# Integer additions of a weight conversion on VectorE, and one block's second product in unsplit float32

## The chip, the cores and the metric

The kernel runs on one core of a Trainium2 chip. What counts is the device time of one launch in microseconds. The engines are TensorE (PE, with its weight loads as PEld), VectorE (DVE), ScalarE (ACT), GpSimd (POOL) and SyncE (SP), which issues most transfers.

## The reference

Three layers follow each other, on 1536 tokens of width 512. The change touches the middle one.

```python
attn_out = _attn_ref(q, k, v)            # 2 x 8 heads, 768 positions: a window of +-15 and 24 block sums
x = attn_out, heads joined               # 1536 x 512
h = x @ w_in                             # 512 x 2048, "first product"
g = where(h > 0, h, exp(min(h, 0)) - 1)
x = g @ w_out                            # 2048 x 512, "second product"
# then a layer of 8 experts, one for each token:
#   e = argmax(x @ w_gate);  out = weight * (relu(x @ w1[e]) @ w2[e])
```

The weights `w_in` and `w_out` arrive in 64-bit floats, and the kernel makes 32-bit ones of them.

## The kernel before

**Blocks and chunks.** The tokens go through attention and the first layer in four blocks of 512, 256, 384 and 384 (`UNITS` counts units of 64 queries). A block j runs over 16 chunks c of 128 hidden columns: `mm_h` (the first product, L422), `elu` (three ScalarE and two VectorE instructions, L433 to L437, with the result `elp`), and, two chunks later, `mm_y` (the second product, L467), which adds into one PSUM bank for each 128 tokens. Attention of the next block's units is put between these steps: scores (L309), the masked maximum (L319), exponent, normalisation (L361), turn (L371), weighted sum (L392), and then the high and the low part of x (`xh` on ScalarE, `xl` on VectorE, L398 and L405). One PSUM buffer `T` serves turns, weighted sums and the means of v.

**Products in parts.** A float32r operand keeps fewer digits than a float32 one. The first product takes x and the weights each as a high and a low part and adds three float32r products. The second product does the same with `split_g` (g into `gh` and `gl`, L447 and L448) and `split_w` (w_out into two parts `wsp`, L175 and L176). In the first block, for chunks below `C3`, it is one float32 product of `elp` and `wo` with no split; there `elp` takes the buffers of `gh` and `gl`, two of each, odd chunks one kind and even chunks the other.

**Conversion.** For each of the 16 chunks both weights are converted, 32 pieces of 128 by 512. A piece takes a ScalarE instruction on the lower half-words (`conv_r`, L127), two VectorE instructions on the upper ones (`conv_t`, L138 and L139), and an integer addition of both (`conv_f`, L146). A piece of w_in then goes through a ScalarE rounding (`conv_h`, L152) and a subtraction (`conv_l`, L157) into high and low part.

**Order.** The start-up is written out by hand in `START`: attention of the first block and the conversion of the first pieces (C00, C01, C10, C20, C30, C11, C21: seven additions; E0 to E3: four subtractions). After it the loop over the 64 steps issues, in each step, the conversion of two pieces, some three chunks ahead of their use; the framework's scheduler puts each engine's instructions of this part into an order by its own timeline, before the run. In the run each engine takes its queue in order. The last block and the experts follow an order of their own.

Of the kernel before, what the change touches and what calls it, by code (L numbers as in the profile page):

```python
# [9 lines left out]
F32 = mybir.dt.float32  # L10
# [5 lines left out]
ALU = mybir.AluOpType  # L16
# [19 lines left out]
BLK = [j for j in range(NBLK) for _ in range(UNITS[j])]  # L36
NF = FF // 128
NS = 6
C3 = 8
WARM = 22  # L40
AT0 = (2, -2, 1)
ATS = (5, 4, 5)
# [14 lines left out]
EXD = (3, 5)  # L57
EXP = (0, 1, 2, 3, 4, 6, 7)
NORMD = (0, 4, 7)
LOE = "VVVPVV"  # L60
START = "w23 w43 x3 w53 w03 w13 w33 w51 x1 w31 w21 w11 w41 w01 w52 x2 w22 w02 w12 w42 w50 x0 w00 w20 w32 d2 d0 w40 d5 k2 s0 w30 d3 k4 k1 k3 s2 k0 k5 m0 w10 s5 m2 e0 s3 m5 M0 e2 m3 d4 M1 r0 b5 d1 b3 s4 n0 e5 r2 t0 e3 m4 n2 s1 c0 z3 e4 M2 z5 t2 r3 r5 M3 n3 c2 m1 A00 M4 n5 B00 e1 M5 k6 r4 C00 n4 t5 P s6 r1 c5 p1 n1 A01 p6 t4 p2 D0 o5 B01 c4 o2 h5 k7 m6 t3 C01 h2 s7 c3 E0 e6 t1 p7 m7 p0 A10 r6 o0 c1 p3 n6 p4 e7 o3 l5 B10 o1 t6 h3 r7 h0 C10 l3 c6 n7 o4 A11 l0 h1 t7 B20 h4 o6 A20 c7 l1 C20 h6 l4 o7 D1 l2 l6 H0 h7 E1 D2 l7 A30 B30 E2 C30 H1 B11 C11 D3 A21 B21 E3 C21"
HID = (5, 10, 15)
LOP = (1, 3, 5, 8, 10, 12, 14)
# [16 lines left out]
class Prog:  # L80
# [60 lines left out]
    def conv_f(self, c, part):  # L141
        t2, r = self.cv.pop((c, part))
        f = t2
        if part == 1:
            f = self.wo[:, c].bitcast(I32)
        self.nc.gpsimd.tensor_tensor(f, t2, r, op=ALU.add)  # L146
        self.w[c, part] = f

    def conv_h(self, c):
# [4 lines left out]

    def conv_l(self, c):
        w, f = self.w[c, 0], self.cvf.pop(c)
        (self.nc.gpsimd if LOE[c % len(LOE)] == "P" else self.nc.vector).tensor_tensor(w[:, 1], f, w[:, 0].bitcast(F32), op=ALU.subtract)  # L157

    def conv_a(self, c, part):
        self.conv_r(c, part)  # L160
# [8 lines left out]
    def split_w(self, j, c):  # L169
        if j == 0 and c < C3:  # L170
            return
        nc = self.nc
        f = self.w[c, 1].bitcast(F32)
        w = self.ws.tile([128, 2, 512], F32R, tag="ws", name="wsp")
        nc.scalar.copy(w[:, 0], f)  # L175
        nc.vector.tensor_tensor(w[:, 1], f, w[:, 0].bitcast(F32), op=ALU.subtract)  # L176
        self.wsp[j, c] = w
# [247 lines left out]
    def elu(self, j, c):  # L425
# [4 lines left out]

        pool, tag = (self.gp, "gh" if c % 2 else "gl") if j == 0 and c < C3 else (self.el, "p")
        p = pool.tile([128, TB], F32, tag=tag, name="elp")[:, :TBS[j]]
# [7 lines left out]
    def split_g(self, j, c):  # L440
        nc = self.nc
        if j == 0 and c < C3:
            return
# [13 lines left out]
    def mm_y1(self, j, c, t):  # L457
        nc = self.nc
        g = self.g[j, c]
        sl = slice(t * 128, t * 128 + 128)  # L460
        if j == 0 and c < C3:
            ops = ((g, self.w[c, 1].bitcast(F32)),)
# [74 lines left out]
    def part1(self):  # L537
# [31 lines left out]
        for x in ORDER.split():  # L569
            f = dict(q=self.load_q, n=self.load_v0, v=self.load_v, w=wload, k=self.load_k0, c=self.load_c)[x[0]]  # L570
            f(int(x[1:]))
        self.new_x(0)
        self.new_x(1)
        self.start_up()
        conv_done = [x for x in pieces if x in self.w]
        del cq[:len(conv_done)]
        while dq and dq[0] in self.split:
# [66 lines left out]
        for i in range(len(steps)):  # L644
            run(2 * i)
            j, c = steps[i]
# [19 lines left out]
    def start_up(self):  # L666

        unit = dict(d=self.diag_q, k=self.k_sum, s=self.scores, m=self.maxes, b=self.less_max, e=self.at1b, z=self.sums, r=self.recip, n=self.norm,
                    t=self.turn, c=self.turned, o=self.weighted, h=self.x_hi, l=self.at5, p=self.v_pad, x=self.max_k0, M=self.mean_v0)
        part = dict(A=self.conv_r, B=self.conv_t, C=self.conv_f)  # L670
        self.split, self.half = set(), set()
        with self.tc.manual_schedule():
            for op in START.split():
                if op[0] == "H":
                    self.mm_h(0, int(op[1:]), 0, TB // 2)
                    self.half.add(int(op[1:]))
                    continue
                k, n = op[0], [int(i) for i in op[1:]]
                if k in unit:
                    unit[k](*n)  # L680
                elif k in part:
                    part[k](*n)
                    if k == "C" and n[1] == 1:
                        self.split.add((n[0], 1))
                elif k == "w":
                    self.window(*n)
                elif k == "P":
                    self.pad_v0()
                elif k == "D":
                    self.conv_h(*n)  # L690
                elif k == "E":
                    self.conv_l(*n)
                    self.split.add((n[0], 0))
# [805 lines left out]
```

## Time and profile before

| | us |
|---|---|
| time, median of 3 runs | 567.46 (567.41 to 567.75) |
| profiled execution, its time | 567.08 |
| its span, first to last instruction | 565.3 |
| busy: TensorE, VectorE, ScalarE, GpSimd | 538.3, 366.3, 311.4, 115.7 |

The profile is of one execution. Times in it are counted from the span's start. A matmul's end is modelled, and matmuls overlap, so that the price of a product is read from the starts of what follows it. The granted clock is that of TensorE, 1.00 being full speed.

### The profile page before, as it was taken

The page shows a single profiled execution, that of the slowest core. Times are in us where ns is not written, and L with a number is a line of the kernel's source. Part 1 is how long each engine was busy: PE and PEld are TensorE (multiplying, and loading weights), DVE is VectorE, ACT ScalarE, POOL GpSimd, SP SyncE. Part 2 cuts the span into 40 slices and gives each one's busy share as a digit, 9 for nine tenths or more (in the row PEclk, how much of TensorE's full clock was granted, in tenths as well). Part 3 has the DMA queues.
Part 4 walks back from the last instruction along what each step waited for, and adds up shares of the span by engine and source line. Part 5 has one row for each costly group of instructions (what it writes and reads, how often), then busy time and mean ns, then how long its engine had stood idle before and what let it go on. Part 6 is the DMA issues. An engine that isn't in the chain of part 4 may idle for free. (4 is left out here: it accounts for less than half of the span.)

```text
span 565.3 us, 9614 instructions
## 1 busy us (share of the span) xinstructions
PE 538.3 (95%) x3113; PEld 422.5 (75%) x3113; DVE 366.3 (65%) x966; ACT 311.4 (55%) x768; POOL 115.7 (20%) x139
## 2 busy tenths in 40 slices
PE   8877998789999999999999999999999999999995
PEld 4465664557889888988888989877888665675884
DVE  6999899997647886787565778885741100444510
ACT  5775564546557877775665754673232222565620
POOL 3656365434000000000000000431432111100001
PEclk9979999889999999999999999998999999999999
DMA  9999733342114130310100101541077979593611
GB/s 291 317 353 399 239 139 105 123 133 52 57 48 138 49 93 16 118 48 14 48 2 1 56 1 50 170 118 56 19 221 267 382 260 370 162 379 131 237 56 40
DMA packets 38714, 81.33 MB, mean 144 GB/s; under 512 B 4095, under 2 KB 8575, under 8 KB 38656
## 3 DMA queue, kind: packets, MB, share of 16 engines
q1 hardware_dynamic: 36336, 73.30, 38.8%
q0 software_dynamic: 2320, 7.34, 3.8%
q8 instruction: 26, 0.43, 0.3%
q14 instruction: 32, 0.26, 0.1%
HBM read 103.70 MB, written 6.55 MB: 195 GB/s over the span
## 5 line engine op out<-in xcount | busy, mean ns | idle before, releaser
L422 PE MATMUL h<-xh,wi 128*128 128x384 f32 (+2 forms) x528 | 144.6, 342 | 0.2 <-ACT elp L435 0.2
L467 PE MATMUL y<-wsp,gh 128*128 128x512 f32 x320 | 100.9, 403 | 0.3
L422 PEld LDWEIGHTS h<-xh,wi 128*128 128x128 f32 x528 | 93.6, 189 | 8.3 <-ACT elp L435 1.0
L422 PE MATMUL h<-xl,wi 128*128 128x384 f32 (+2 forms) x264 | 88.0, 333 | 0.0
L467 PEld LDWEIGHTS y<-wsp,gh 128*128 128x128 f32 x320 | 58.2, 191 | 10.5 <-ACT gh L447 1.1
L467 PE MATMUL y<-wsp,gl 128*128 128x512 f32 x160 | 62.3, 405 | 1.3 <-DVE gl L448 1.3
L1157 DVE TENSOR_TENSOR holdl<-S,holdh 128x512 fp32r<-128x512 f32 x22 | 15.2, 689 | 72.1 <-ACT holdh L1153 53.7
L1125 PE MATMUL h<-w2s,holdh 128*128 128x512 f32 x176 | 61.0, 407 | 0.0
L1168 PE MATMUL y<-w2s,holdh 128*128 128x512 f32 x176 | 59.1, 398 | 0.0
L436 DVE SCALAR_TENSOR_TENSOR elt<-ele,elt 128x384 f32<-128x384 f32 (+2 forms) x64 | 41.3, 646 | 19.5 <-ACT ele L434 19.1
L422 PEld LDWEIGHTS h<-xl,wi 128*128 128x128 f32 x264 | 49.9, 189 | 4.5 <-issue 1.2
L433 ACT ACTIVATE elt<-h 128x384 f32<-128x384 f32 (+2 forms) x64 | 31.4, 491 | 28.5 <-PE h L422 23.0
L447 ACT CAST gh<-elp 128x384 fp32r<-128x384 f32 (+2 forms) x56 | 27.8, 496 | 31.9 <-DVE elp L437 22.0
L176 DVE TENSOR_TENSOR wsp<-wo,wsp 128x512 fp32r<-128x512 f32 x56 | 39.9, 713 | 8.2 <-ACT wsp L175 7.5
L437 DVE SCALAR_TENSOR_TENSOR elp<-elt,elp 128x384 f32<-128x384 f32 (+2 forms) x64 | 41.8, 652 | 3.9
L175 ACT CAST wsp<-wo 128x512 fp32r<-128x512 f32 x56 | 34.7, 620 | 15.4 <-PE y L467 13.8
L1125 PEld LDWEIGHTS h<-w2s,holdh 128*128 128x128 f32 x176 | 33.9, 192 | 8.3 <-issue 0.8
L336 ACT ACTIVATE e<-e,nb 128x120 f32<-128x120 f32 x88 | 33.7, 389 | 10.4 <-DVE nb L324 10.2
L1168 PEld LDWEIGHTS y<-w2s,holdh 128*128 128x128 f32 x176 | 33.1, 188 | 8.4 <-issue 1.6
L448 DVE TENSOR_TENSOR gl<-elp,gh 128x384 fp32r<-128x384 f32 (+2 forms) x56 | 31.0, 554 | 12.1 <-ACT gh L447 10.8
L467 PEld LDWEIGHTS y<-wsp,gl 128*128 128x128 f32 x160 | 29.9, 190 | 8.4 <-DVE gl L448 2.5
L1125 PE MATMUL h<-w2s,holdl 128*128 128x512 f32 x88 | 35.0, 398 | 0.0
(290 smaller groups left out, 973.1 us busy)
## 6 DMA issues: line engine op xcount, KB each, us to landing
wo<-in_w SPq DMA_DIRECT2D x9, 2048.0 KB
wo<-in_w SPq DMA_DIRECT2D x18, 1024.0 KB
ri<-in_w_in SPq DMA_DIRECT2D x16, 512.0 KB
ro<-in_w_out SPq DMA_DIRECT2D x16, 512.0 KB
wo<-in_w SPq DMA_DIRECT2D x32, 256.0 KB
w2p<-in_w SPq DMA_DIRECT2D x32, 256.0 KB
w2q<-in_w SPq DMA_DIRECT2D x24, 256.0 KB
q<-in_q SPq DMA_DIRECT2D x18, 256.0 KB
```

Source lines behind the costliest of these rows:

```text
L175: nc.scalar.copy(w[:, 0], f)
L176: nc.vector.tensor_tensor(w[:, 1], f, w[:, 0].bitcast(F32), op=ALU.subtract)
L336: nc.scalar.activation(e[:, p], e[:, p], AF.Exp, bias=nb[:, p:p + 1], scale=0.125, accum_out=sm[:, p:p + 1])
L422: nc.tensor.matmul(h, lhsT=w[:, wl, k * 128:k * 128 + 128], rhs=x[:, k, a:b], start=(n == 0), stop=(n == 11))
L433: nc.scalar.activation(t, h, AF.Tanh, scale=0.5)
L436: nc.vector.scalar_tensor_tensor(t, e, 1.0, t, op0=ALU.add, op1=ALU.mult)
L437: nc.vector.scalar_tensor_tensor(p, t, 0.0, p, op0=ALU.min, op1=ALU.add)
L447: nc.scalar.copy(gh, p)
L448: nc.vector.tensor_tensor(gl, p, gh.bitcast(F32), op=ALU.subtract)
L467: nc.tensor.matmul(self.y[j][t], lhsT=gx[:, sl], rhs=wx, start=(c == 0 and n == 0), stop=(c == NF - 1 and n == len(ops) - 1))
L1125: nc.tensor.matmul(self.h[s, hf], lhsT=x[:, k], rhs=w, start=(n == 0), stop=(n == 11))
L1168: nc.tensor.matmul(self.y2[s], lhsT=g[:, ks], rhs=w, start=(i == 0 and n == 0), stop=(i == 7 and n == 2))
```

## The change

`C3` goes from 8 to 16, so that the first block's second product is one float32 product in all 16 chunks, with no split of g and of w_out there. The integer addition of a conversion is made on VectorE instead of GpSimd, but for the seven of the start-up. The subtractions of the conversion that were on GpSimd (chunks 3, 9 and 15, the first of them in the start-up) are made on VectorE like the others.

```diff
-C3 = 8
+C3 = 16
...
-LOE = "VVVPVV"
...
     def conv_f(self, c, part):
...
-        self.nc.gpsimd.tensor_tensor(f, t2, r, op=ALU.add)
+        (self.nc.gpsimd if self.early else self.nc.vector).tensor_tensor(f, t2, r, op=ALU.add)
         self.w[c, part] = f
...
     def conv_l(self, c):
         w, f = self.w[c, 0], self.cvf.pop(c)
-        (self.nc.gpsimd if LOE[c % len(LOE)] == "P" else self.nc.vector).tensor_tensor(w[:, 1], f, w[:, 0].bitcast(F32), op=ALU.subtract)
+        self.nc.vector.tensor_tensor(w[:, 1], f, w[:, 0].bitcast(F32), op=ALU.subtract)
...
         self.start_up()
+        self.early = False
...
-        self.split, self.half = set(), set()
+        self.split, self.half, self.early = set(), set(), True
```

## Rows read from the trace of the kernel before

**Rows 1.** The page: its span, and busy time, share and instructions of VectorE.

```profile
span 565.3 us, 9614 instructions
...
PE 538.3 (95%) x3113; PEld 422.5 (75%) x3113; DVE 366.3 (65%) x966; ACT 311.4 (55%) x768; POOL 115.7 (20%) x139
```

**Rows 2.** Busy time by stretches: from:to, length, engines (instructions), clock, DMA, GB/s.

```profile
53.00:140.00 87.00, 77.73 (x331) 50.82 (x332) 80.77 (x140) 51.20 (x117) 40.51 (x29) 0.94 0.44 144
...
55.00:60.00 5.00, 5.00 (x13) 2.69 (x12) 4.90 (x8) 4.37 (x14) 3.04 (x3) 0.73 1.04 297
...
75.00:80.00 5.00, 5.00 (x21) 2.93 (x20) 5.00 (x9) 1.71 (x3) 2.67 (x2) 1.00 0.32 105
...
100.00:105.00 5.00, 3.72 (x15) 3.02 (x16) 4.96 (x7) 2.83 (x6) 2.59 (x2) 0.70 0.20 45
...
120.00:125.00 5.00, 3.05 (x10) 2.33 (x11) 5.00 (x11) 1.60 (x4) 0.54 (x1) 0.75 0.27 82
```

**Rows 3.** VectorE's groups from 53 to 140 us: busy us, mean ns.

```profile
L437 DVE SCALAR_TENSOR_TENSOR elp<-elt,elp 128x512 f32<-128x512 f32 x12 | 14.4, 1202 | 0.5
L157 DVE TENSOR_TENSOR wi<-cv_t,wi 128x512 fp32r<-128x512 f32 x10 | 12.7, 1267 | 0.0
...
L138 DVE TENSOR_SCALAR cv_t<-ri 128x512 int32<-128x512 int32 x12 | 5.0, 416 | 0.0
```

**Rows 4.** VectorE in order of time: start us, length us, instruction.

```profile
80.14 0.68 DVE L139 SCALAR_TENSOR_TENSOR cv_t<-ri,cv_t 128x512 int32<-128x512 int32 x1
80.75 1.78 DVE L157 TENSOR_TENSOR wi<-cv_t,wi 128x512 fp32r<-128x512 f32 x1
82.45 1.78 DVE L436 SCALAR_TENSOR_TENSOR elt<-ele,elt 128x512 f32<-128x512 f32 x1
```

**Rows 5.** GpSimd in order of time, the same moments.

```profile
80.36 1.61 POOL L146 TENSOR_TENSOR wo<-cv_t,cv_r 128x512 int32<-128x512 int32 x1 [1.97 <-DVE cv_t L139]
81.94 1.74 POOL L146 TENSOR_TENSOR cv_t<-cv_t,cv_r 128x512 int32<-128x512 int32 x1
```

**Rows 6.** TensorE in order of time: an unsplit second product and what follows it.

```profile
75.75 3.59 PE L467 MATMUL y<-wo,elp 128*128 128x512 f32 x8
79.18 1.05 PE L309 MATMUL S<-k,q 128*128 128x120 f32 x8
80.06 0.60 PE L371 MATMUL T<-c,e 128*120 128x128 f32 x4
80.42 0.48 PE L422 MATMUL h<-xh,wi 128*128 128x512 f32 x1
```

**Rows 7.** TensorE in order of time: a first product's start, then a split second product's.

```profile
132.83 0.39 PE L422 MATMUL h<-xh,wi 128*128 128x512 f32 x1
...
135.55 0.61 PE L467 MATMUL y<-wsp,gh 128*128 128x512 f32 x2
```

**Rows 8.** TensorE in order of time: the phase's ends and its stops.

```profile
53.24 5.37 PE L467 MATMUL y<-wo,elp 128*128 128x512 f32 x8 [3.16 <-DVE elp L437]
...
101.28 0.65 PE L371 MATMUL T<-c,e 128*120 128x128 f32 x4 [4.40 <-DVE xl L405]
...
111.13 0.69 PE L392 MATMUL T<-et,v 120*64 120x64 f32 x16 [1.14 <-ACT et L378]
...
120.84 0.50 PE L467 MATMUL y<-wsp,gl 128*128 128x512 f32 x1 [1.27 <-DVE gl L448]
...
122.68 1.11 PE L371 MATMUL T<-c,e 128*120 128x128 f32 x4 [1.11 <-DVE xl L405]
...
172.01 0.28 PE L422 MATMUL h<-xh,wi 128*128 128x256 f32 x1
```

**Rows 9.** TensorE's groups from 53 to 172 us: the mean products.

```profile
L236 PE MATMUL T<-c,vn 128*128 128x4 f32 x48 | 5.8, 244 | 0.9 <-DVE xl L405 0.9
```

**Rows 10.** GpSimd's groups from 53 to 140 us: the additions.

```profile
L146 POOL TENSOR_TENSOR cv_t<-cv_t,cv_r 128x512 int32<-128x512 int32 x12 | 18.9, 1578 | 20.1 <-DVE cv_t L139 8.2 <-ACT cv_r L127 5.9 <-ACT wsp L175 3.5
L146 POOL TENSOR_TENSOR wo<-cv_t,cv_r 128x512 int32<-128x512 int32 x12 | 17.6, 1469 | 20.1 <-DVE cv_t L139 8.0 <-ACT wi L152 4.5 <-issue 3.4
```

## The prediction

> **What bounds the kernel now.** I read the page first: VectorE is busy 366.3 us of the 565.3 us span, far from a bound as an average [rows 1]. An average says nothing here, so the next view is the busy time in short stretches. From 53 to 140 us VectorE is busy 80.8 of 87 us, and in a middle stretch 5.00 of 5.00, while GpSimd is busy 40.5 us [rows 2]. This is the stretch in which the first block goes through the first layer and in which most weights are converted. TensorE looks full there too, but its spans are stretched, so I measure it by starts instead.
>
> Prices by starts, at full clock. A second product of an unsplit chunk starts at 75.75 and what follows it at 79.18: 3.43 us for four token tiles. The scores of one unit take 0.88 us, a turn 0.36 us [rows 6]. A first product of one chunk, twelve float32r matmuls of 512 columns, runs from 132.83 to 135.55: 2.72 us [rows 7]. A split second product is also twelve such matmuls, so it costs 2.72 us too.
>
> The phase of the first block lasts from the first second product at 53.24 to the end of the last one, which the next block's matmul at 172.01 marks: 118.8 us [rows 8]. Its work: 8 unsplit products, 27.4 us; 8 split ones, 21.8; 13 first products, 35.4; the second block's first two, half as wide, 2.7; five scores 4.4; four turns 1.4; four weighted sums at 0.69 [rows 8], 2.8; 48 mean products, 5.8 [rows 9]. Sum 101.7 us. So 17.1 us of the phase are lost, and every microsecond of them delays all that follows, because TensorE is the engine that all later blocks queue on.
>
> Where they are lost: the marked stops at 101.28, 111.13, 120.84 and 122.68 are 4.40 + 1.14 + 1.27 + 1.11 = 7.9 us, three of them released by VectorE (the low part of x twice, gl once) and one by ScalarE [rows 8]. After a stop TensorE runs slow: the granted clock is 0.70 from 100 to 105 us and 0.75 from 120 to 125 [rows 2]. With only a full level and a half level (2.4 and 1.2 GHz), 0.70 is 3.0 us at the half one, which loses 1.5 us, and 0.75 loses 1.25. The stretch 55 to 60 us, after the start-up's stop of 3.16 us [rows 8], has 0.73 and loses 1.4. The rest, 17.1 - 7.9 - 2.8 - 1.4 = 5.0 us, is spread thin.
>
> Why VectorE is late is seen when it is laid beside GpSimd. GpSimd adds from 80.36 to 81.97 and from 81.94 to 83.68 [rows 5]. VectorE's instructions at 80.75 and 82.45, of the shape that takes 0.68 us at 80.14, take 1.78 us and end with GpSimd's plus their own work [rows 4]. So one addition on GpSimd costs VectorE up to 1.1 us. The Trainium skill, SBUF — State Buffer, section Who interferes with whom, says that a VectorE instruction with two SBUF inputs and a GpSimd instruction that reads SBUF exclude each other for a whole instruction; the trace agrees, 0.68 against 1.78 us.
>
> **The change, part by part.** *Additions.* GpSimd loses 24 additions between 53 and 140 us, 36.5 us [rows 10], and two subtractions (chunks 9 and 15); by the code 32 - 7 = 25 additions follow the start-up, so one lies just before. It was not the bound, so its own time is worth nothing; the blocking is. At most 26 x 1.1 = 28.6 us of VectorE's time go. At least what two groups show: L437 has 12 at 1.202 us, L157 10 at 1.267 [rows 3], against 0.68: 6.3 + 5.9 = 12.2 us. I take 20, the middle. VectorE gains 24 additions and two subtractions. No row shows an integer addition there; the nearest is the integer instruction of 512 elements at 80.14, which lets the next start 0.61 us later [rows 4]. Its bounds are 0.33 us (L138, 0.416 us less the same overlap [rows 3]) and GpSimd's 1.47 to 1.58 [rows 10]. I take 0.60: 15.6 us.
>
> *Splits.* Eight weight splits and eight splits of the activations go from both ScalarE and VectorE, all in this phase; 7 of VectorE's 16 lie before 140 us, 4.2 us. VectorE's load from 53 to 140 becomes 80.8 - 20 - 4.2 + 15.6 = 72.2 us. ScalarE is busy 51.2 of the 87 us [rows 2], so its part counts nothing; if it were the pace, two instructions a chunk would go, some 1.4 us at VectorE's 0.68.
>
> *TensorE.* Eight chunks change from 2.72 to 3.43 us: +0.71 each, 5.7 us, all on the engine that sets the end. That is the certain cost, 2.1 us before 140 us and 3.6 after, where TensorE has few gaps to absorb it. The bounds are narrow, since both forms are in the trace: 5.4 to 6.0. A page would make it more: the Trainium skill, FP8 and Floating Point Precision, section TensorE Precision Notes, gives true float32 four passes; counting each float32r product as one, that is four against three, an estimate of 0.91 us a chunk and 7.3 us in all. The rows measure 3.43 against 2.72, and the measurement decides.
>
> *Buffers.* The activations of chunks 8 to 15 move to the two gh and two gl buffers, which the splits leave free. A buffer comes round every four chunks and a second product lags two, so nothing waits; if it did, the cost would be one second product, 3.4 us, once. The weight ring also loses eight split tiles; transfers get room, and DMA is at 0.44 [rows 2], so 0. *Start-up:* one subtraction moves from GpSimd to VectorE: +0.6 against up to 1.1 us less blocking; I take 0, between -0.5 and +0.6.
>
> *What comes back.* If VectorE no longer comes late, the 7.9 us of stops and the 2.8 us of low clock behind them go. TensorE needs about 77.7 - 4.1 + 2.1 = 75.7 us of work between 53 and 140 (busy time less the low clock's 1.5 + 1.25 + 1.4, plus three chunks' float32 [rows 2]), VectorE 72.2: 95%. That is close, and both queues run in order, so I keep one stop of 1.2 us with 0.6 us of low clock, and take back a quarter of the thin losses, 1.2 us. Recovered: 7.9 + 2.8 - 1.8 + 1.2 = 10.1 us; bounds 0 (all stops persist) and 15.7 (everything but the first low clock).
>
> *Sum*, against the profiled execution (567.08 us, its span 565.3 and 1.8 around it): 567.1 - 10.1 + 5.7 = 562.7. The median is 0.4 higher, so I say 563.0. The later blocks keep their work and move forward whole.
>
> **The rivals.** (1) VectorE stays the pace: its additions stand ahead of the short instructions that TensorE waits for, and about half of the losses stay. For it: 95%, and an order that is planned, not measured. Against it: without the blocking hardly a VectorE instruction is longer than 0.7 us, so what stands in front of a short one is halved. Recovered 5.5, paid 5.7: 567 us, no change.
> (2) The other side: an integer addition on VectorE takes GpSimd's time, or the order is worse, and nothing is recovered. The deciding point: VectorE's load equals TensorE's when 57.8 + 24d = 75.7 (72.2 less the 24 additions at 0.60 is 57.8), d = 0.75 us; with d = 1.5 it is 93.8 us, 18 more than TensorE's and 6.8 more than the stretch lasts now. Then 567.1 + 5.7 and up to 6.8: 573 to 580 us. For it: no row of an integer addition on VectorE. Against it: every VectorE instruction of two sources and 512 elements takes near 0.68 us where GpSimd is still, integers and floats alike.
> (3) Everything is recovered, the start-up's stop too: 567.1 - 15.7 + 5.7 = 557 us. Against it: in-order queues and the small bound of VectorE.
>
> **How the numbers follow.** A median of this kernel can be told from no change at about 0.2%, 1.1 us. The forecast, -2 to -8 us, has 0.66; rival 1, within 0.2% or just past it, 0.13, of which 0.11 counts as same; rival 2 has 0.14; rival 3 has 0.07. Faster 0.75, same 0.11, slower 0.14. The range runs from 556.8, rival 3, to 568.2, where rival 1 ends and rival 2 alone is left out with a little below. The likeliest case's own range is 559 to 565.
>
> **What would show it.** In the changed profile: no addition on GpSimd after the start-up; additions of about 0.69 us on VectorE; L157 and L437 back at 0.68 to 0.7 us instead of 1.2; VectorE below 5.00 of 5 us between 75 and 95; the stops of 4.40 and 1.27 us gone, with a granted clock of 1.00 there; 64 more records of the unsplit second product at the price of 3.43 us a chunk; and the phase shorter by some 4 us. The prediction is wrong if the addition is much over 0.75 us, if TensorE's stops return at other instructions, or if the unsplit product runs slower than the rows say once eight more stand in a row.

## The result, and the profile after

The changed kernel takes 560.12 us (median of 4 runs, 558.94 to 560.79) beside 567.43 us for the kernel before in the same session: ratio 0.9868, 95% interval 0.9849 to 0.9887. The forecast was 563.0. The line numbers of the changed kernel are lower by one in this part: L466 is the L467 of before, L436 the L437, L145 the L146.

The page after: the span, and the busy time of the engines.

```profile
span 556.8 us, 9493 instructions
...
PE 538.1 (97%) x3081; PEld 414.5 (74%) x3081; DVE 347.7 (62%) x978; ACT 304.2 (55%) x752; POOL 72.8 (13%) x111
```

TensorE is as busy as before [rows 1], in a span that is 8.5 us shorter. The stretches after, with the columns of [rows 2]:

```profile
53.00:140.00 87.00, 87.00 (x365) 54.44 (x364) 75.24 (x166) 53.35 (x122) 1.78 (x3) 0.98 0.46 149
...
55.00:60.00 5.00, 5.00 (x16) 3.01 (x16) 5.00 (x11) 3.90 (x9) 0.00 (x0) 0.84 1.04 283
...
75.00:80.00 5.00, 5.00 (x21) 2.87 (x19) 5.00 (x11) 3.79 (x7) 0.00 (x0) 1.00 0.37 119
...
100.00:105.00 5.00, 5.00 (x32) 3.29 (x31) 5.00 (x13) 4.03 (x13) 0.00 (x0) 1.00 0.43 145
...
120.00:125.00 5.00, 5.00 (x33) 3.39 (x32) 4.86 (x10) 2.86 (x6) 1.51 (x2) 1.00 0.46 132
```

From 53 to 140 us TensorE is now busy all the 87 us, where it was 77.7, and its clock is 1.00 where it had been 0.70 and 0.75. VectorE is still full between 75 and 80 us, but each of its instructions has its own length again, and it finishes 11 of them there instead of 9. Its groups from 53 to 140 us (busy us, mean ns):

```profile
L436 DVE SCALAR_TENSOR_TENSOR elp<-elt,elp 128x512 f32<-128x512 f32 x14 | 9.6, 685 | 0.3
...
L145 DVE CUSTOM_DVE_ANT_0 cv_t<-cv_t,cv_r 128x1024 uint16<-128x1024 uint16 x12 | 8.2, 686 | 0.0
L145 DVE CUSTOM_DVE_ANT_0 wo<-cv_t,cv_r 128x1024 uint16<-128x1024 uint16 x12 | 8.2, 684 | 0.6 <-ACT cv_r L126 0.4
...
L156 DVE TENSOR_TENSOR wi<-cv_t,wi 128x512 fp32r<-128x512 f32 x12 | 8.1, 678 | 0.1
```

L436 falls from 1202 to 685 ns and L156 from 1267 to 678 [rows 3]. The added integer additions take 685 ns.

TensorE in order of time: the first second product and what follows it, one in the middle with its successor, and the end of the phase.

```profile
52.19 5.37 PE L466 MATMUL y<-wo,elp 128*128 128x512 f32 x8 [2.46 <-DVE elp L436]
56.99 0.79 PE L421 MATMUL h<-xh,wi 128*128 128x512 f32 x1
...
74.69 3.60 PE L466 MATMUL y<-wo,elp 128*128 128x512 f32 x8
78.13 1.05 PE L308 MATMUL S<-k,q 128*128 128x120 f32 x8
...
158.13 3.60 PE L466 MATMUL y<-wo,elp 128*128 128x512 f32 x8
161.16 0.68 PE L421 MATMUL h<-xh,wi 128*128 128x256 f32 x1
161.68 0.28 PE L421 MATMUL h<-xl,wi 128*128 128x256 f32 x1
...
172.83 0.20 PE L524 MATMUL y<-wg,mab 128*128 128x48 bf16 x1 [1.53 <-ACT mab L511]
...
377.81 2.42 PE L530 MATMUL y<-rc,mt 128*128 128x16 f32 x21
```

Between 52.19 and 161.16 us no idle time is marked: the four stops of [rows 8] are gone, and a fifth of 0.91 us at 138.89 [rows 9]. The phase is 109.0 us long instead of 118.8. Its end mark lies 0.4 us early, because the float32r product behind an unsplit one takes that much longer to its successor (161.16 to 161.68, 0.12 elsewhere), so it is 109.4 by work. Its work by the prediction's prices is 101.7 + 5.7 us, less 1.0 for one of the six groups of mean products, which now comes after the mark: 106.4. So 3.0 us are lost, and 1.7 of them are the first second product at low clock: 4.80 us from 52.19 to 56.99, as in the kernel before, against 3.11 at full clock before the same successor in the kernel with C3 = 12 below.

The phase begins 1.05 us earlier. That is not shown to be the change's doing: the runs below with additions on VectorE after the same start-up begin it between 51.88 and 54.07 us. At 172.83 TensorE waits 1.53 us for ScalarE at the hand-over to the second block, a stop that was not there before. In the middle blocks the changed kernel is 7.80 us ahead of the kernel before, at the last block's gate product 8.3 (377.81 above). TensorE's rows at the same products, first of the kernel before, then one of the changed kernel:

```profile
287.73 0.34 PE L422 MATMUL h<-xl,wi 128*128 128x384 f32 x1
...
386.10 2.08 PE L531 MATMUL y<-rc,mt 128*128 128x16 f32 x18
```

```profile
279.93 0.34 PE L421 MATMUL h<-xl,wi 128*128 128x384 f32 x1
```

### The profile page after: what moved, and what is told of

It reads as the page before. It is cut to its first block, busy times and chain, and to the rows that moved or that the text cites. A ratio compares the mean times of both kernels' runs of the same rounds, so it can differ in the third digit from the quotient of the medians.

```text
span 556.8 us, 9493 instructions
## 1 busy us (share of the span) xinstructions
PE 538.1 (97%) x3081; PEld 414.5 (74%) x3081; DVE 347.7 (62%) x978; ACT 304.2 (55%) x752; POOL 72.8 (13%) x111
## 5 line engine op out<-in xcount | busy, mean ns | idle before, releaser
L466 PE MATMUL y<-wsp,gh 128*128 128x512 f32 x256 | 78.4, 399 | 0.4 <-ACT gh L446 0.4
L466 PE MATMUL y<-wo,elp 128*128 128x512 f32 x128 | 60.2, 609 | 2.5 <-DVE elp L436 2.5
L435 DVE SCALAR_TENSOR_TENSOR elt<-ele,elt 128x384 f32<-128x384 f32 (+2 forms) x64 | 37.1, 580 | 34.4 <-ACT ele L433 33.9
L466 PEld LDWEIGHTS y<-wsp,gh 128*128 128x128 f32 x256 | 46.0, 188 | 8.2 <-ACT gh L446 0.9
L466 PE MATMUL y<-wsp,gl 128*128 128x512 f32 x128 | 48.5, 402 | 0.0
L466 PEld LDWEIGHTS y<-wo,elp 128*128 128x128 f32 x128 | 24.3, 194 | 26.1 <-issue 25.0
L175 DVE TENSOR_TENSOR wsp<-wo,wsp 128x512 fp32r<-128x512 f32 x48 | 33.9, 706 | 7.3 <-ACT wsp L174 7.2
L436 DVE SCALAR_TENSOR_TENSOR elp<-elt,elp 128x384 f32<-128x384 f32 (+2 forms) x64 | 35.5, 554 | 3.3
L174 ACT CAST wsp<-wo 128x512 fp32r<-128x512 f32 x48 | 29.8, 621 | 12.7 <-PE y L466 12.3
L1168 PE MATMUL y<-w2s,holdl 128*128 128x512 f32 x88 | 34.4, 391 | 0.0
```

Source lines behind the costliest of these rows:

```text
L435: nc.vector.scalar_tensor_tensor(t, e, 1.0, t, op0=ALU.add, op1=ALU.mult)
L436: nc.vector.scalar_tensor_tensor(p, t, 0.0, p, op0=ALU.min, op1=ALU.add)
L466: nc.tensor.matmul(self.y[j][t], lhsT=gx[:, sl], rhs=wx, start=(c == 0 and n == 0), stop=(c == NF - 1 and n == len(ops) - 1))
L1168: nc.tensor.matmul(self.y2[s], lhsT=g[:, ks], rhs=w, start=(i == 0 and n == 0), stop=(i == 7 and n == 2))
```

## The experiments

Two theories stood at first. The prediction's: GpSimd's additions hold VectorE up, and the unsplit product is a pure price. The rival's: the gain comes from the sixteen splits that are dropped, or from a chain that no longer runs through GpSimd.

**One half alone: unsplit products only.** The kernel before with

```diff
-C3 = 8
+C3 = 16
```

> The kernel before with C3 = 16 alone; all additions and subtractions stay where they were. Blocking theory (GpSimd's additions hold VectorE up, and the unsplit product costs TensorE 5.7 us): the price is paid and only the splits' share of VectorE's load goes (4.2 us before 140 us), so 568 to 573 us, slower than before. Rival (the gain comes from the splits that are dropped): 559 to 563 us, like the whole change.

Measured 571.78 us, ratio 1.0088 (1.0059 to 1.0117): slower than before. Three of the four stops of [rows 8] stand at the same instructions; the fourth, for `gl`, went with the splits. TensorE's rows of this kernel in order of time:

```profile
103.30 1.11 PE L371 MATMUL T<-c,e 128*120 128x128 f32 x4 [4.40 <-DVE xl L405]
...
113.14 0.69 PE L392 MATMUL T<-et,v 120*64 120x64 f32 x16 [1.35 <-ACT et L378]
...
124.08 0.66 PE L371 MATMUL T<-c,e 128*120 128x128 f32 x4 [1.19 <-DVE xl L405]
```

Dropping the splits does not bring the gain; this half of the change loses 5 us by itself.

**The other half alone: additions and subtractions only.** The changed kernel with

```diff
-C3 = 16
+C3 = 8
```

> The changed kernel with C3 back at 8: only additions and subtractions are moved. Blocking theory: no unsplit product more is paid (-5.7 us against the whole change), but VectorE carries 4.2 us of splits more before 140 us and comes to some 79 us of 87, so 2 to 4 us of stops return: 556 to 559 us. Rival (the dropped splits are the gain): 565 to 568 us.

Measured 552.39 us, ratio 0.9762 (0.9713 to 0.9811), 7.7 us under the whole change and 3.6 under the bottom of what I expected: no stop returned. VectorE carries its splits without harm, busy 81.35 of the 87 us:

```profile
53.00:140.00 87.00, 87.00 (x403) 60.87 (x402) 81.35 (x188) 59.53 (x140) 3.09 (x4) 0.98 0.46 147
```

That is more than the 80.8 of the kernel before, in the same stretch [rows 2], and TensorE is busy throughout. So the busy share does not tell whether VectorE is late: in the same busy time it finishes 188 instructions here and 140 in the kernel before, where they are stretched.

**Blocking without a chain.** The changed kernel, with an addition on GpSimd after each later piece whose result nobody reads:

```diff
+        self.idle = c.tile([128, 512], BF16, name="idle")
...
         self.w[c, part] = f
+        if part == 1 and not self.early:
+            self.load_pool(f)
+
+    def load_pool(self, f):
+        f = f.bitcast(F32)
+        self.nc.gpsimd.tensor_tensor(self.idle, f, f, op=ALU.add)
...
         self.w[c, 0] = w
+        if not self.early:
+            self.load_pool(w[:, 0])
```

> The changed kernel, and for each of the 25 later pieces GpSimd also makes one addition of 128x512 from the finished weight into a tile that nobody reads; no engine waits for it. Blocking theory: 25 times up to 1.1 us come back onto VectorE without a longer chain, the stops return, 567 to 574 us. Rival (the gain is the shorter chain, without the hand-over to GpSimd): nobody waits for GpSimd, so 559 to 562 us.

Measured 566.31 us, ratio 0.9984 (0.9963 to 1.0006): 6.2 us come back over the changed kernel, to just under the range expected (567 to 574). VectorE's additions stretch from 686 to 887 ns, L445 (the L436 above) from 685 to 820, and TensorE's stops return. VectorE's groups from 53 to 140 us, and TensorE's stops in order of time:

```profile
L146 DVE CUSTOM_DVE_ANT_0 cv_t<-cv_t,cv_r 128x1024 uint16<-128x1024 uint16 x12 | 10.6, 887 | 0.0
L445 DVE SCALAR_TENSOR_TENSOR elp<-elt,elp 128x512 f32<-128x512 f32 x12 | 9.8, 820 | 0.1
```

```profile
99.69 0.62 PE L379 MATMUL T<-c,e 128*120 128x128 f32 x4 [1.34 <-ACT wi L158]
...
120.26 0.65 PE L379 MATMUL T<-c,e 128*120 128x128 f32 x4 [1.28 <-DVE xl L413]
...
138.46 1.05 PE L244 MATMUL T<-c,vn 128*128 128x4 f32 x8 [1.94 <-DVE xl L413]
```

None of these three waits is for GpSimd itself. The work on GpSimd reaches TensorE through VectorE and ScalarE. It does not bring back all that moving the additions is worth at C3 = 16, which is 571.78 - 560.12 = 11.7 us. The dose is smaller too: with each group's mean length less that of the same instruction in the changed kernel, times its count, VectorE loses some 16 us here from 53 to 140 us, and some 23 in the kernel before (estimates).

**Half of that dose.** The same without the second call, 13 idle additions instead of 25:

```diff
-        if not self.early:
-            self.load_pool(w[:, 0])
```

> The changed kernel with an idle addition on GpSimd after each w_out piece only, 13 of the 25. Blocking theory: half of the 6 us that the 25 cost, some 562 to 564.5 us. Rival (a threshold: nothing shows until VectorE is full): 559 to 561 us.

Measured 559.78 us, ratio 0.987 (0.9842 to 0.9898): nothing. So the cost is not in proportion; the rival, a threshold, is right here. Half of the blocking disappears in the room that VectorE has. In the changed kernel that room is 87 - 75.2 = 11.8 us; the 13 idle additions stretch VectorE's instructions by some 7 us, the 25 by some 16 (estimates, as above). The stretch with 13, then with 25:

```profile
53.00:140.00 87.00, 86.50 (x359) 53.99 (x359) 82.92 (x168) 54.14 (x122) 26.30 (x16) 0.98 0.49 159
```

```profile
53.00:140.00 87.00, 81.37 (x338) 50.14 (x339) 86.16 (x160) 49.11 (x112) 38.28 (x26) 0.98 0.45 151
```

**Load without blocking.** The changed kernel with each later addition made twice:

```diff
+        if not self.early:
+            self.nc.vector.tensor_tensor(f, t2, r, op=ALU.add)
         self.w[c, part] = f
```

> The changed kernel with each later addition made twice on VectorE (for w_in the lower part is then added twice, so its last digits change). The load argument of the prediction (VectorE near TensorE's time between 53 and 140 us): 24 x 0.6 = 14.4 us more on VectorE, 75 to 90 us in a stretch where TensorE has some 76 us of work, so at least half of it shows: 566 to 574 us. Rival (VectorE has room once nothing blocks it): only 0.7 us on the chain of a piece that is converted three chunks ahead, 559 to 562 us.

Measured 558.97 us, ratio 0.986 (0.9827 to 0.9892): nothing, a miss for the prediction's load argument. The stretch from 53 to 140 us, and the 10 us behind it:

```profile
53.00:140.00 87.00, 87.00 (x362) 53.76 (x361) 83.83 (x191) 51.37 (x117) 1.71 (x4) 0.98 0.45 145
...
140.00:150.00 10.00, 10.00 (x55) 7.60 (x54) 7.85 (x16) 4.63 (x16) 0.39 (x1) 1.00 0.53 176
```

VectorE is busy 83.8 us, 3 more than in the kernel before, and TensorE never stands still in that stretch. Of the added work, 23 instructions or some 14 us at 0.60, part fills VectorE's room and part moves other work behind 140 us: of the next 10 us VectorE is busy 7.85, where it is 3.46 in the changed kernel.

```profile
140.00:150.00 10.00, 10.00 (x48) 6.85 (x47) 3.46 (x14) 3.25 (x12) 0.27 (x1) 1.00 0.15 48
```

By size this load is near that of the 25 idle additions, which cost 6 us. These additions each take their 0.68 us and the order of the queues was planned with them; whether that or the last few microseconds of load make the difference, no run here separates.

**Blocking with C3 = 8.** To see how much of the first half's gain the chain through GpSimd could be, the 25 idle additions were put into the kernel with C3 = 8:

> Additions on VectorE, C3 = 8, and the 25 idle additions on GpSimd. VectorE then has the blocking of the kernel before and the additions besides, but no piece's chain runs through GpSimd. If blocking alone made the kernel before slow: 567 us or more. If the chain through GpSimd (the addition's 1.5 us and its hand-overs) was part of it: well below, 558 to 563 us, and what is missing to 567 is at least the chain's part.

Measured 569.0 us, ratio 1.0041 (1.0019 to 1.0063): with the additions on VectorE and the blocking back, all of the gain of 15 us is gone. It is not a clean split, for two reasons that its rows show. VectorE carries the additions too, and one stop of 3.88 us is for GpSimd itself, for the copies of block sums that the scores need. The idle addition ahead of them ended at 132.97; two copies, 0.27 us each when alone, then took 5.96. TensorE's rows, then GpSimd's:

```profile
99.49 0.62 PE L379 MATMUL T<-c,e 128*120 128x128 f32 x4 [3.06 <-ACT wi L158]
...
139.25 2.06 PE L317 MATMUL S<-k,q 128*128 128x120 f32 x8 [3.88 <-POOL k L305]
```

```profile
128.87 4.10 POOL L153 TENSOR_TENSOR idle<-wo 128x512 bf16<-128x512 f32 x1 [1.37 <-DVE wo L146]
133.44 5.96 POOL L305 COPY k<-ks 128x96 f32<-128x96 f32 x2 [0.48 <-issue]
```

Without that stop some 565 us would be left, near the kernel before. So blocking, with the additions besides, is enough to undo most of the gain; how much of the 15 us was blocking and how much the chain through GpSimd stays open. At C3 = 16 blocking alone gave back 6.2 of 11.7 us, at a smaller dose. The chain is seen once to reach TensorE: in the kernel before VectorE stands still for a subtraction on GpSimd, and TensorE's fifth stop follows. VectorE's row, then TensorE's:

```profile
136.88 0.43 DVE L138 TENSOR_SCALAR cv_t<-ro 128x512 int32<-128x512 int32 x1 [3.21 <-POOL wi L157]
```

```profile
138.89 1.06 PE L236 MATMUL T<-c,vn 128*128 128x4 f32 x8 [0.91 <-DVE xl L405]
```

**Where the best C3 lies.** Four more kernels with the additions on VectorE, each with one number changed.

C3 = 0:

> Additions on VectorE and C3 = 0: no unsplit product at all in the first block. If each unsplit product costs 0.71 us on TensorE and VectorE's load does not matter, 16 x 0.71 = 11.4 us under the whole change, 5.7 under C3 = 8: 547 us. If VectorE's load does matter, eight splits more (9.6 us) in a stretch where it is busy 81 of 87 us make stops, and it comes to 550 to 555 us.

C3 = 4:

> Additions on VectorE and C3 = 4. By TensorE's price alone 2.8 us under C3 = 8 (552.4): 549.5 us. If VectorE's load already costs at C3 = 8, the same as C3 = 8 or a little more: 552 to 554 us.

C3 = 6:

> Additions on VectorE and C3 = 6. TensorE's price: 1.4 us under C3 = 8, 551 us. If the loss seen at C3 = 4 (557.1) and 0 (560.8) is that of VectorE's and ScalarE's splits, it has begun here too: 553 to 556 us.

C3 = 12:

> Additions on VectorE and C3 = 12. If TensorE's price of 0.71 us a chunk is all that divides C3 = 8 from 16 (552.4 and 560.1), then 2.8 us over C3 = 8 and 2.8 under the whole change: 555 to 557 us. If some step of the order between 8 and 16 does it, at one of the two ends.

| C3 | us | ratio to before, 95% interval |
|---|---|---|
| 0 | 560.79 | 0.9887 (0.9853 to 0.9921) |
| 4 | 557.09 | 0.9805 (0.9776 to 0.9833) |
| 6 | 554.6 | 0.9795 (0.9745 to 0.9845) |
| 8 | 552.39 | 0.9762 (0.9713 to 0.9811) |
| 12 | 553.85 | 0.9766 (0.9738 to 0.9794) |
| 16 | 560.12 | 0.9868 (0.9849 to 0.9887) |

C3 = 6 came out in its second range and 12 near the time of C3 = 8, one of the two ends that it named; 0 and 4 are slower than either range that I expected. TensorE's price alone would make 0 the best by 5.7 us over 8. It is the slowest, level with 16 within the intervals: splits of the first chunks stand in the start-up's chain, as the first second product of C3 = 0 shows.

```profile
56.98 3.78 PE L466 MATMUL y<-wsp,gh 128*128 128x512 f32 x8 [5.83 <-ACT gh L446]
```

With 0, 4 and 6 TensorE also stops for the block sums, 2.31, 2.13 and 2.58 us. With C3 = 4 two of GpSimd's copies take 5.27 us, where the changed kernel's first two take 1.51 and a lone one 0.27; VectorE runs one instruction after the other meanwhile, its splits among them. TensorE's stop, then GpSimd's copies:

```profile
134.73 2.06 PE L308 MATMUL S<-k,q 128*128 128x120 f32 x8 [2.13 <-POOL k L296]
```

```profile
129.62 5.27 POOL L296 COPY k<-ks 128x96 f32<-128x96 f32 x2 [64.65 <-DVE ks L221]
136.92 0.27 POOL L296 COPY k<-ks 128x96 f32<-128x96 f32 x1 [2.03 <-issue]
```

So the same sharing of the two engines, the other way round, is a likely reason for the loss below 8; no run takes these copies off GpSimd.

From 8 to 12 the step is too small to be told from none, and from 12 to 16 it is 6 us, where the price is 2.8 each time. In the profiled executions part of that unevenness is seen at C3 = 12: its first second product runs at full clock, though it stands behind the same stop as the changed kernel's and that of C3 = 8, shown second.

```profile
52.85 3.67 PE L466 MATMUL y<-wo,elp 128*128 128x512 f32 x8 [2.46 <-DVE elp L436]
55.96 0.80 PE L421 MATMUL h<-xh,wi 128*128 128x512 f32 x1
...
168.42 0.20 PE L524 MATMUL y<-wg,mab 128*128 128x48 bf16 x1 [0.77 <-ACT mab L511]
```

```profile
51.88 5.37 PE L466 MATMUL y<-wo,elp 128*128 128x512 f32 x8 [2.47 <-DVE elp L436]
56.69 0.80 PE L421 MATMUL h<-xh,wi 128*128 128x512 f32 x1
```

That saves it 1.7 us against both, and its stop at the hand-over is 0.8 us shorter than at 16.

**The start-up's additions on VectorE too**, with C3 = 8:

```diff
-        (self.nc.gpsimd if self.early else self.nc.vector).tensor_tensor(f, t2, r, op=ALU.add)
+        self.nc.vector.tensor_tensor(f, t2, r, op=ALU.add)
```

> Additions on VectorE, those of the start-up too, and C3 = 8. Blocking theory: seven additions of 1.27 to 1.6 us on GpSimd go, which hold VectorE up by some 1.1 us each, against 0.6 us each on VectorE; the start-up's order is written by hand and VectorE is full there, so 1 to 3 us earlier: 549 to 552 us. Rival (the start-up waits for transfers and for its own chain): 552 to 554 us.

Measured 551.4 us, ratio 0.9734 (0.9681 to 0.9787). The stop before the first second product is gone, but 1.25 us of waiting appear at 117.05, and the interval overlaps that of C3 = 8 alone. Both beat the kernel before and the changed kernel; between the two nothing is decided.

**The three subtractions back on GpSimd**, with C3 = 8:

```diff
-        self.nc.vector.tensor_tensor(w[:, 1], f, w[:, 0].bitcast(F32), op=ALU.subtract)
+        (self.nc.gpsimd if c % 6 == 3 else self.nc.vector).tensor_tensor(w[:, 1], f, w[:, 0].bitcast(F32), op=ALU.subtract)
```

> As with C3 = 8 and the additions on VectorE, but the subtractions of chunks 3, 9 and 15 stay on GpSimd. Blocking theory: three blocks of some 1.1 us and a chain longer by 0.8 us, one of them ahead of the first second product, so 1 to 2 us over 552.4. Rival (three instructions are nothing): 552 to 553 us.

Measured 553.32 us, ratio 0.9745 (0.9705 to 0.9785): no difference that can be told. Three blocks are nothing, as 13 are nothing.

## Why the prediction was right, and what was mis-sized

**The place and the mechanism held.** The phase from the first to the last second product of the first block was where time was lost, and GpSimd's additions were what made VectorE late: moved to VectorE they free 15 us (C3 = 8) or some 12 (C3 = 16), and idle work on GpSimd at C3 = 16 takes 6 of these away. The Trainium skill's rule in SBUF — State Buffer, section Who interferes with whom, that a VectorE instruction with two SBUF inputs and a GpSimd instruction that reads SBUF exclude each other, is borne out by VectorE additions that depend on nothing of GpSimd's and still take 887 instead of 686 ns. Of the blocking I took 20 us; by the estimate above it was some 23. What blocking leaves of the gain, about half at C3 = 16 with the smaller dose, may be the chain.

**TensorE's price held.** The unsplit product takes 3.44 us in the changed kernel (74.69 to 78.13) against 3.43 forecast, and the whole change is slower than its first half by 7.7 us in the medians, 6 by the ratios, against 5.7. Undone, this part of the change would bring about as much again as the whole change brought.

**The integer addition held**, at 0.685 us long and 0.60 apart, and the deciding point of 0.75 us was not even one: at two additions a piece nothing is lost. The second rival is out by that.

**What was mis-sized is the term "what comes back".** I kept one stop of 1.2 us with its low clock and took back a quarter of the thin losses, 10.1 us in all. The losses themselves were a little smaller than my sum: it left out one turn (L243, 0.35 us at 168.35), so that 16.7 us were lost and not 17.1, and the first low clock cost 1.7 and not 1.4, since it began before 55 us. The phase recovered 16.7 - 3.0 = 13.7: every stop, all of the low clock behind them, and some 3.0 of the 4.3 us that are left as thinly spread, 0.91 of them the fifth stop, which I had not counted as one. What the rest of the thin losses were is not shown. The reason for keeping some was VectorE at 95% of TensorE's time between 53 and 140 us. Its load came out at 75.2 against 72.2 forecast, but the argument fell with the doubled additions, 83.8 us and no stop. The stretch was the wrong frame: pieces are converted three chunks ahead, and VectorE's work can slip behind 140 us, where it has room. One of the signs that I had named failed: between 75 and 95 us VectorE is as full as before, 19.86 of 20 us against 19.93, and yet TensorE does not stop. Another was too small: the phase is 9.4 us shorter, not some 4.

**What was missed on the other side** is 1.5 us: the stop at 172.83, where TensorE waits for ScalarE. The start-up, taken as 0, shows 1.05, which lies within what it varies by between runs. Together: -1.05 - 13.7 + 5.7 + 1.5 = -7.6, where the changed kernel is 7.8 ahead in the middle blocks and the profiled executions differ by 567.08 - 558.94 = 8.1. The medians differ by 7.3, because the profiled execution is the fastest of four that spread over 1.9 us. That the forecast is only 2.9 us off is in part luck: the recovery was 3.6 too small, and the missed stop took back 1.5.

**Rival 1** (half of the losses stay) and **rival 3** (all recovered, 557 us) both named the recovery as the open term; 13.7 us lies nearer to rival 3's 15.7 than to the forecast's 10.1, and the time, 560.1, midway between the two. What stays open is how much of VectorE's lateness was blocking and how much the chain through GpSimd, and how much of the cost is the planned order of the queues, which in the kernel before reckoned with instructions of their undisturbed length: no run here separates a late order from a full engine.

## What to carry to other kernels

When one engine's instructions of one shape show two lengths, here 0.68 and 1.78 us, lay them beside the neighbour that shares something with them; the neighbour's own idle time hides the cost. When a change has two halves, price each on its own engine: here one half was worth 15 us and the other cost about 6, and the sum looked like a success. A busy share near 100% tells little when work can be done ahead of its use or when instructions are stretched: count the instructions beside it (140 and 188 in the same busy time here), and double the suspected load, which is a cheap test.

## What the runs showed of the hardware that was not expected

The integer addition of 512 32-bit numbers stands in VectorE's trace as a custom instruction over 1024 16-bit ones, and takes 685 ns, like the float subtraction of the same tile (678).

The exclusion works the other way too. In the kernel with C3 = 8 and idle additions, one addition on GpSimd, which takes 1.36 us a moment earlier, takes 7.43 while VectorE runs one instruction after the other at its own length; the copies of block sums above, 0.27 us alone and over 5 for two, are the case where TensorE pays for it. GpSimd and VectorE of that kernel in order of time:

```profile
91.27 1.36 POOL L153 TENSOR_TENSOR idle<-wo 128x512 bf16<-128x512 f32 x1 [2.56 <-issue]
...
98.30 7.43 POOL L153 TENSOR_TENSOR idle<-wo 128x512 bf16<-128x512 f32 x1 [3.29 <-issue]
```

```profile
99.27 0.68 DVE L444 SCALAR_TENSOR_TENSOR elt<-ele,elt 128x512 f32<-128x512 f32 x1
...
102.94 0.68 DVE L146 CUSTOM_DVE_ANT_0 wo<-cv_t,cv_r 128x1024 uint16<-128x1024 uint16 x1
```

After a stop of 2.46 us at the same instruction TensorE ran at half its clock for a while in the changed kernel (the first second product took 4.80 us to its successor) and at full clock with C3 = 12 (3.11). What TensorE did before was nearly the same; no run here tells what decides it.
